# A planner's rules for shared PSUM banks and for reserved buffers, with a new list of seeds for the order of an attention stage

## Chip, cores and metric

The kernel runs on one core of a Trainium2 chip. The metric is the device time of one execution in microseconds (us); lower is better. Times are given as the median of several executions. The profile is one execution more, taken with the hardware profiler.

## The reference

Attention with a causal mask, and then two layers of matrix products with an elementwise function between the two products of each, all in fp32:

```python
scores = scale * np.matmul(q, k.transpose(0, 1, 3, 2))      # (2, 12, 448, 64) each
scores = np.where(mask, -1000000000.0, scores)
attn = np.exp(scores - np.max(scores, axis=-1, keepdims=True))
attn = attn / (np.sum(attn, axis=-1, keepdims=True) + 1e-09)
attn_out = np.matmul(attn, v)
x = attn_out.transpose(0, 2, 1, 3).reshape(896, 768)
h = x @ w_in;  x = (h * np.clip(h + 3.0, 0.0, 6.0) / 6.0) @ w_out            # 768 -> 2048 -> 768
h = x @ w2_in; y = (np.maximum(h, 0.0) + alpha * np.minimum(h, 0.0)) @ w2_out
```

## The kernel before, in words

**The two stages.** The first stage is attention. `attend` (L408) is called once for each of six groups `c`; a group has two halves, and each half (`chunks`, L497) holds two heads, one on each 64 rows of the core, called sides. TensorE (PE) makes the scores of a half in three steps (`score`, L512, tiles `s01` and `s2` of PSUM) and those of the last 64 rows of both halves of a group in one step (L436, tile `sl`). VectorE (DVE) adds the mask and takes the highest score (L463), ScalarE (ACT) takes the exponentials (L468), DVE or GpSimd (POOL) adds a constant to the sums (L483), DVE takes reciprocals (L485), and POOL or DVE scales the rows (L492; `SCALERS` = 2 leaves ACT out). PE then transposes blocks into three tiles `t` a half (L537) and, from the last rows, into two tiles `r` a group (L448). ACT or DVE copies each `t` (L563) and, for each half, its part of each `r` (L570) into the tile `a`. PE multiplies the values by `a` into a PSUM tile `o` (L581). `take_x` (L351) makes sums and differences of the `o` tiles and splits them into high and low halves (L297, L299 the high one; L303, L306 the low one), the inputs of the second stage.

The second stage is the four matrix products, each with seven block products in place of eight. All its matmuls stand on L600 in groups of three (high by high, high by low, low by high), in an order that a chain fixes. Weights arrive as 64-bit words and are turned into fp32 on ACT and DVE (L278, L281, L284). Sums of weights are made on DVE (L325) or by an accumulating DMA that POOL issues (L323).

**What sets the order.** Nothing is ordered by hand. Each step of the program is an `Op` (L50) with the engines it may run on, a duration for each, a due time, the buffers it uses and the operations that must come before it. `Plan.solve` (L117) places them one after the other: for each engine it looks at the operations that are ready, works out the earliest time `t` at which each could start (L175 to L189), and of all engines takes the earliest. Both the order on each engine and the engine of an operation that may run on several come out of this. A buffer is an object of class `Buf` (L43) and gets a slot of its class when an operation that names it is placed (L230); the slots are 8 banks of PSUM (`ps`), 12 tiles `e` and so on (`SLOTS`, L838). Before the change an operation could start only when the slot that it takes was free in time (L189), also where it only reserves the buffer for a later operation (the argument `also` of `Plan.op`, L91): the score steps on PE reserve the tile `e` that DVE writes later (L517, L519), the last-row scores reserve `el` (L440), and the transposes reserve `a` (L555). Buffers are followed by part: two engines that use different parts of one PSUM tile were not ordered by the plan. The program that is built from the plan takes a tile at the first operation that names its buffer (L888 to L902), and the framework beneath puts in the semaphores, for PSUM tiles by whole tile.

The due times of the attention operations are shifted at random by a list of seeds (`SEEDS`, L844; L131 to L142); each seed also may fix an operation to one of its engines. The first seed shifts all operations, and the others a share.

Of the kernel before, what the change touches and what calls it, by code (L numbers as in the profile page):

```python
# [42 lines left out]
class Buf:  # L43

    def __init__(self, cls, name, cols=None, dtype=None):
        self.cls, self.name, self.cols, self.dtype = cls, name, cols, dtype
        self.left, self.end, self.slot, self.tile = 0, 0.0, None, None


class Op:  # L50
# [17 lines left out]
LAG = {PE: 0.20, DVE: 0.12, ACT: 0.15, POOL: 0.10, SP: 0.04}  # L68
# [17 lines left out]
class Plan:  # L86
# [4 lines left out]
    def op(self, on, emit, reads=(), writes=(), due=FAR, chain=None, also=(), port=False, mode=None):  # L91
# [7 lines left out]
        for key in writes:  # L99
# [2 lines left out]
            o.before.update(r)  # L102
            self.state[key] = ([o], [])
        o.before.discard(o)
        for key in (*reads, *writes, *also):
            b = key[0] if isinstance(key, tuple) else key
            if b not in o.bufs:
                o.bufs.append(b)
                b.left += 1
# [7 lines left out]
    def solve(self, slots, strict, overlay, vary=0, seeds=()):  # L117
# [51 lines left out]
        while len(done) < len(self.ops):  # L169
            best = None  # L170
            room = {c: queue[c][:len(free[c])] for c in strict}
            for e in LAG:
                can = []
                for o in ready[e]:
# [7 lines left out]
                    for b in o.bufs:  # L182
                        if b.slot is None:
                            need[b.cls] = need.get(b.cls, 0) + 1
                            f = free[b.cls]
                            if len(f) < need[b.cls] or (b.cls in room and b not in room[b.cls]):
                                ok = False
                                break
                            t = max(t, sorted(f)[need[b.cls] - 1][0])  # L189
                    if ok and len(o.on) > 1:  # L190
                        def done_by(x, us):
                            late = max(clock[x], o.ready[x], port if (x == POOL and x not in o.dma) or (x == DVE and o.port) else 0.0)
# [37 lines left out]
            for b in [b for b in o.bufs if b.slot is None]:  # L230
                f = free[b.cls]
                k = min(range(len(f)), key=lambda i: f[i][0])
                b.slot = f.pop(k)[1]
                if b.cls in strict:
                    queue[b.cls].remove(b)
            for b in o.bufs:
                b.left -= 1
                b.end = max(b.end, o.out + LAG[e])
                if not b.left:
                    free[b.cls].append((b.end, b.slot))  # L240
# [600 lines left out]
SPLIT = (0, 1)  # L841
SEND = 0
SCALERS = 2
SEEDS = (13117, 66982, 68691, 27780, 6959, 27726, 88620, 72214, 67132, 73300, 90690, 68978, 52530, 59003, 43003)  # L844
ATT = {"kq": 2 * S, "v": 8 * D, "e": 3 * P, "el": 4 * P, "small": 21, "a": 16 * P}


# [5 lines left out]
def fused_kernel(ctx: ExitStack, tc: tile.TileContext, dram):  # L853
# [21 lines left out]
    with tc.manual_schedule():  # L875
# [11 lines left out]
            nc.gpsimd.memset(t[:, S:], 0.0)  # L887
        for o in order:  # L888
            for b in o.bufs:
                if b.tile is not None:  # L890
                    continue
                if b.cls == "el":
                    b.tile = last[b.slot]
# [62 lines left out]
```

## Time and profile before

| what | us |
|---|---|
| time, median of 3 runs (lowest to highest) | 500.47 (497.64 to 500.74) |
| time of the profiled execution | 497.29 |
| its span, from the first to the last instruction | 495.4 |
| PE busy in that span | 484.7 |
| mean granted clock of PE, as a share of full | 0.999 |

The span is what the trace shows; the profiled execution took 1.9 us more than its span. PE's busy time is the sum of its matmuls, whose ends are modelled. "Idle before" in a row is the time for which the engine stood before that instruction, and the name after the arrow is what ended it. The view of waits gives, for each engine, the sum of such times by line.

### The profile page before, as it was taken

What the parts mean: (1) busy time and instruction counts of PE and PEld (TensorE: products, weight loads), DVE (VectorE), ACT (ScalarE), POOL (GpSimd) and SP (SyncE); (2) the same over time, 40 slices, a digit from 0 to 9 for tenths busy, and PEclk for the clock granted to TensorE, in tenths of its full rate; (3) what the DMA queues carried; (4) which work ended last, traced back from release to release, by engine and by line L of the source; (5) the groups of instructions that cost most, each with busy time, mean ns of one, the idle gap of its engine ahead of it and who ended that gap; (6) DMA issues with size and microseconds to landing.
All of it is one profiled execution on the core that took longest, in us unless ns stands there. A gap on an engine that the chain in (4) does not pass through costs nothing.

```text
span 495.4 us, 7593 instructions
## 1 busy us (share of the span) xinstructions
PE 484.7 (98%) x2596; PEld 426.9 (86%) x2596; DVE 430.8 (87%) x823; ACT 388.4 (78%) x755; POOL 115.5 (23%) x182
## 2 busy tenths in 40 slices
PE   8899898999999999999999999999999999999997
PEld 4566576899999999999999999999999999999996
DVE  5697997999999899999999999998789988999810
ACT  5999999878989899868984578898788977697201
POOL 3767475200005001470001000121320014700000
PEclk9999999999999999999999999999999999999999
DMA  8754410334558957999105035675594689970111
GB/s 272 304 167 134 142 40 1 127 129 155 176 195 230 282 160 233 239 271 271 30 0 160 1 128 180 209 198 161 164 230 153 200 245 258 233 137 1 57 56 56
DMA packets 25334, 79.08 MB, mean 160 GB/s; under 512 B 2896, under 2 KB 13136, under 8 KB 25296
## 3 DMA queue, kind: packets, MB, share of 16 engines
q1 hardware_dynamic: 15216, 61.76, 36.3%
q0 software_dynamic: 10080, 16.85, 19.3%
q8 instruction: 20, 0.33, 0.3%
q14 instruction: 18, 0.15, 0.1%
HBM read 59.00 MB, written 2.75 MB: 125 GB/s over the span
## 4 chain that ended last, share of the span: by engine, by line
PE 91%; ACT 4%; DVE 4%; issue 1%; POOL 0%; DVEq 0%; ACTq 0%
PE ya L600 24%; PE a L600 23%; PE yc L600 12%; PE c L600 11%; PE yb L600 6%; PE b L600 6%; PE t L537 3%; PE o L581 3%; PE s L512 3%; ACT e L468 2%; ACT a L563 1%; PE warm L819 1%; DVE e L463 1%; DVE e L492 1%; PE r L448 1%
## 5 line engine op out<-in xcount | busy, mean ns | idle before, releaser
L284 DVE SCALAR_TENSOR_TENSOR wf<-wf,raw 128x768 uint32<-128x768 uint32 x64 | 60.5, 951 | 4.4 <-ACT wf L278 4.0
L323 POOL DMA_DIRECT2D g<-g x46 | 41.3, 1308 | 95.4 <-DVE x70l L306 18.6
L278 ACT ACTIVATE wf<-raw 128x768 f32<-128x768 f32 x64 | 57.9, 906 | 6.7 <-PE yc L600 3.4
L281 ACT ACTIVATE raw<-raw 128x768 uint32<-128x768 uint16 x64 | 58.6, 915 | 0.8 <-DMA raw<-w1o 0.8
L323 POOL DMA_DIRECT2D wf<-wf x17 | 16.1, 979 | 161.7 <-ACT r L676 52.2
L468 ACT ACTIVATE e<-e,small 128x384 f32<-128x384 f32 (+2 forms) x72 | 36.0, 510 | 6.2 <-DVE small L463 5.9
L463 DVE CUSTOM_DVE_ANT_0 e<-s,mask 128x384 f32<-128x384 f32 (+2 forms) x72 | 26.4, 417 | 7.6 <-PE s L512 5.5
L492 POOL TENSOR_SCALAR e<-e,small 128x256 f32<-128x256 f32 (+2 forms) x65 | 30.1, 480 | 10.9 <-DVE small L485 5.6
L581 PEld LDWEIGHTS o<-a,v 128*64 128x64 f32 x192 | 12.6, 136 | 14.0 <-issue 4.9
L581 PE MATMUL o<-a,v 128*64 128x448 f32 (+3 forms) x192 | 23.0, 385 | 1.5 <-ACT a L563 1.3
L335 ACT COPY o<-ya 128x448 f32<-128x448 f32 x3 | 1.6, 532 | 28.2 <-PE ya L600 28.2
L512 PE MATMUL s<-kq 64*128 64x256 f32 (+2 forms) x144 | 21.1, 413 | 1.0 <-DMA kq<-kq 0.7
L512 PEld LDWEIGHTS s<-kq 64*128 64x128 f32 x144 | 13.3, 195 | 9.5 <-DVE small L463 4.2
L325 DVE TENSOR_TENSOR wf<-wf 128x768 f32<-128x768 f32 (+1 forms) x23 | 19.1, 829 | 0.2
L537 PE MATMUL t<-ident,e 128*128 128x128 f32 x144 | 19.0, 277 | 0.3 <-DVE small L483 0.3
L682 ACT ACTIVATE r<-g 128x448 f32<-128x448 f32 x24 | 13.8, 575 | 6.4 <-DVE g L666 6.2
L634 DVE TENSOR_TENSOR s12l<-s,s12h 128x768 fp32r<-128x768 f32 x16 | 15.2, 951 | 3.5 <-ACT s12h L633 3.5
L676 ACT ACTIVATE r<-g 128x448 f32<-128x448 f32 x24 | 13.7, 573 | 5.6 <-DVE g L666 5.6
L537 PEld LDWEIGHTS t<-ident,e 128*128 128x128 f32 x144 | 15.6, 141 | 2.6 <-POOL e L492 1.8
L634 DVE TENSOR_TENSOR s<-wf,s 128x384 fp32r<-128x384 f32 x32 | 16.8, 548 | 0.0
L633 ACT CAST a1h<-wf 128x768 fp32r<-128x768 f32 x16 | 13.4, 837 | 3.7 <-DVE wf L284 3.6
L684 DVE SCALAR_TENSOR_TENSOR g<-r,alpha,g 128x448 f32<-128x448 f32 x24 | 16.3, 678 | 0.0
(835 smaller groups left out, 1754.5 us busy)
## 6 DMA issues: line engine op xcount, KB each, us to landing
raw<-w1i SPq DMA_DIRECT2D x16, 768.0 KB, 4.7
raw<-w1o SPq DMA_DIRECT2D x16, 768.0 KB, 5.6
raw<-w2i SPq DMA_DIRECT2D x16, 768.0 KB, 4.6
raw<-w2o SPq DMA_DIRECT2D x16, 768.0 KB, 5.7
g<-g POOLq DMA_DIRECT2D x46, 224.0 KB, 8.0
kq<-kq SPq DMA_DIRECT2D x11, 448.0 KB, 4.1
v<-v SPq DMA_DIRECT2D x12, 256.0 KB, 3.3
wf<-wf POOLq DMA_DIRECT2D x8, 384.0 KB, 10.1
```

The lines of the kernel that those rows point to most:

```text
L278: op((ACT, 0.80), lambda e: nc.scalar.activation(f32(w.tile), f32(words(1)), AF.Prelu, scale=sign * 2.0 ** -112, alpha=-2.0 ** 32), reads= ...
L281: op((ACT, 0.81), lambda e: nc.scalar.activation(words(0), raw.tile.bitcast(U16).rearrange("p (n four) -> p n four", four=4)[:, :, 1], AF. ...
L284: op((DVE, 0.87), lambda e: nc.vector.scalar_tensor_tensor(out=w.tile, in0=w.tile, scalar=3, in1=words(0), op0=ALU.logical_shift_left, op1 ...
L323: nc.gpsimd.dma_start(out=dst(), in_=src(), accum_op=ALU.add)
L463: nc.vector.tensor_tensor_reduce(out=view(), in0=t.tile[:, off:off + cols], in1=self.mask[:, at:at + cols], scale=-SCALE, scalar=3.0e38, o ...
L468: nc.scalar.activation(view(), view(), AF.Exp, bias=small.tile[:, u:u + 1], scale=-1.0, accum_out=small.tile[:, 7 + u:8 + u])
L492: (nc.gpsimd if e == POOL else nc.vector).tensor_scalar(view(), view(), by, 1.0, ALU.mult, ALU.mult)
L512: nc.tensor.matmul(t.tile[:, off:off + (i + 1) * P], lhsT=kq.tile[rows, S + i * P:S + (i + 1) * P], rhs=kq.tile[rows, 0:(i + 1) * P], star ...
L537: nc.tensor.transpose(t.tile[:, at * P:(at + 1) * P], src.tile[:, off:off + P], self.ident)
L581: nc.tensor.matmul(o.tile[side * D:(side + 1) * D, 0:cols], lhsT=v.tile[:, (2 * kc + side) * D:(2 * kc + side + 1) * D], rhs=a.tile[:, at: ...
L600: nc.tensor.matmul(out, lhsT=t.tile[:, first + at:first + at + P], rhs=rhs.tile, start=start and key is hi and rhs is xh, stop=stop and ke ...
L634: op((DVE, 0.065 + 0.00105 * cols), lambda _: nc.vector.tensor_sub(out(1), src(), f32(out(0))), reads=[*keys, parts[0][0]], writes=[parts[ ...
```

## The change

Three things change in the planner, and one in how its plan is written out. A buffer that an operation only reserves (the set `held`) still needs a slot, but its time is no longer waited for; the operation that first uses it waits for the time at which the slot came free (`b.free`). A PSUM buffer keeps, for each engine, the end of that engine's last use (`b.used`), and an operation on another engine is placed behind that end. A tile is taken at the first operation that uses its buffer, not at one that reserves it. The list of seeds is another one.

```diff
@@ class Buf
         self.left, self.end, self.slot, self.tile = 0, 0.0, None, None
+        self.free, self.used = 0.0, {}
@@ Plan.op
         o.before.discard(o)
+        o.held = {key[0] if isinstance(key, tuple) else key for key in also}
@@ Plan.solve
-                            t = max(t, sorted(f)[need[b.cls] - 1][0])
+                            if b not in o.held:
+                                t = max(t, sorted(f)[need[b.cls] - 1][0])
+                        elif b not in o.held:
+                            t = max(t, b.free)
+                        for x, end in b.used.items():
+                            if x != e:
+                                t = max(t, end + LAG[x])
@@ Plan.solve
-                b.slot = f.pop(k)[1]
+                b.free, b.slot = f.pop(k)
...
             for b in o.bufs:
+                if b.cls == "ps":
+                    b.used[e] = o.out
@@
-SEEDS = (13117, 66982, 68691, 27780, 6959, 27726, 88620, 72214, 67132, 73300, 90690, 68978, 52530, 59003, 43003)
+SEEDS = (13117, 66982, 68691, 27780, 6959, 88620, 72214, 67132, 73300, 90690, 68978, 52530, 43003, 92613, 49163, 31964, 54657, 49905, 53656, 67591, 13047, 17716, 1373, 15352, 49387, 3553, 56373, 97534, 14618, 44146, 634, 7068, 79464, 72678, 226)
@@ fused_kernel
-                if b.tile is not None:
+                if b.tile is not None or b in o.held:
                     continue
```

The lines of the changed kernel stand ten further down than those of the kernel before (L512 becomes L522, L537 L547, L581 L591, L600 L610, L563 L573, L570 L580, L448 L458, L436 L446).

The first place is PE in the middle of attention, from the fifth of the six last-row scores (`sl`) to the product `o` behind it. Before:

```order
L436 MATMUL sl<-kq 64x448 x4
L512 MATMUL s_760<-kq 128x256
L512 MATMUL s_761<-kq 128x256
L512 MATMUL s_760<-kq 128x128
L512 MATMUL s_761<-kq 128x128
L448 MATMUL r<-ident,el 128x128 x8
L537 MATMUL t<-ident,e_621 128x128
L537 MATMUL t<-ident,e_630 128x128
```

And in the changed kernel:

```order
L446 MATMUL sl<-kq 64x448 x4
L547 MATMUL t<-ident,e_616 128x128
L547 MATMUL t<-ident,e_647 128x128
L547 MATMUL t<-ident,e_631 128x128
L547 MATMUL t<-ident,e_642 128x128
L458 MATMUL r<-ident,el 128x128 x8
L547 MATMUL t<-ident,e_647 128x128
L547 MATMUL t<-ident,e_616 128x128
```

The four score matmuls between `sl` and the transposes `r` have moved behind the products `o`, and the first four of twelve transposes `t` now stand in their place.

The second place is DVE at the same time, with the rows that stand beside those of PE. Before:

```order
L563 COPY a<-t 128x2x256
L492 TENSOR_SCALAR el<-el,small 128x448
L492 TENSOR_SCALAR e_621<-e_621,small 128x128
L492 TENSOR_SCALAR e_621<-e_621,small 128x256
L463 ISA el,small<-sl,mask 128x448
L463 ISA small 128x1
L463 ISA el,small<-sl,mask 128x448
```

And in the changed kernel:

```order
L573 COPY a<-t 128x2x256
L502 TENSOR_SCALAR el<-el,small 128x448
L473 ISA el,small<-sl,mask 128x448
L473 ISA small 128x1
L473 ISA el,small<-sl,mask 128x448
L473 ISA small 128x1
L294 SCALAR_TENSOR_TENSOR wf<-wf,raw 128x768
```

The two scalings of a tile `e` that stood between the scaling of `el` and the reading of `sl` are gone from here: in the changed kernel one of them stands earlier on DVE and the other is on POOL.

The third place is PE at the end of attention, from the last four transposes `t` to the last product `o`. Before:

```order
L537 MATMUL t<-ident,e_1019 128x128
L537 MATMUL t<-ident,e_1028 128x128
L537 MATMUL t<-ident,e_1020 128x128
L537 MATMUL t<-ident,e_1023 128x128
L600 MATMUL a<-t201h,s12h 128x448
L600 MATMUL a<-t201l,s12h 128x448
L600 MATMUL a<-t201h,s12l 128x448
L581 MATMUL o<-a,v 64x448 x2
```

And in the changed kernel:

```order
L547 MATMUL t<-ident,e_1068 128x128
L547 MATMUL t<-ident,e_1098 128x128
L547 MATMUL t<-ident,e_1075 128x128
L547 MATMUL t<-ident,e_1086 128x128
L591 MATMUL o<-a,v 64x448 x2
L591 MATMUL o<-a,v 64x320 x2
L591 MATMUL o<-a,v 64x192 x2
L591 MATMUL o<-a,v 64x64 x2
```

The three matmuls of the second stage that stood between the last transposes and the last `o` have moved ahead; in the changed kernel the last `o` and the one before it each follow their own transposes directly.

## Rows read from the trace of the kernel before

**Rows 1.** The page, its head and its first part (busy time, share, instructions).

```profile
span 495.4 us, 7593 instructions
...
PE 484.7 (98%) x2596; PEld 426.9 (86%) x2596; DVE 430.8 (87%) x823; ACT 388.4 (78%) x755; POOL 115.5 (23%) x182
```

**Rows 2.** Busy time by stretch: stretch, length, each engine's busy us (instructions), clock, DMA, GB/s.

```profile
80.00:90.00 10.00, 8.69 (x62) 6.54 (x59) 9.39 (x17) 9.38 (x19) 4.40 (x5) 1.00 0.17 46
...
100.00:150.00 50.00, 50.00 (x248) 46.26 (x248) 49.00 (x82) 41.83 (x70) 0.90 (x1) 1.00 0.50 170
...
sum 95.00, PE 87.77 PEld 60.07 DVE 77.03 ACT 84.78 POOL 56.01; mean PE 4.62 PEld 3.16 DVE 4.05 ACT 4.46 POOL 2.95
```

**Rows 3.** Waits of PE in the whole span: us in total, times, longest.

```profile
PE r L448 <- POOL el L492: 1.8, 3, 1.1
PE o L581 <- ACT a L563: 1.3, 1, 1.3
PE warm L819 <- DVE mask L877: 1.3, 1, 1.3
PE r L448 <- DVE small L463: 1.1, 1, 1.1
PE s L512 <- DMA kq<-kq: 0.7, 1, 0.7
PE s L512 <- DVE small L463: 0.4, 2, 0.2
PE a L600 <- DVE a L634: 0.3, 1, 0.3
PE t L537 <- DVE small L483: 0.3, 1, 0.3
PE o L581 <- issue: 0.2, 1, 0.2
```

**Rows 4.** Waits of ACT and of DVE in the first 95 us, those between the two.

```profile
ACT a L570 <- DVE a L570: 1.2, 1, 1.2
...
ACT b2202h L297 <- DVE t L348: 0.6, 1, 0.6
...
DVE a L570 <- ACT e L468: 1.7, 1, 1.7
...
DVE t L348 <- ACT b2202h L297: 0.6, 1, 0.6
```

**Rows 5.** Timeline, 49 to 61 us: start, us, engine, line, operation, tiles, count [idle before].

```profile
49.63 0.87 DVE L492 TENSOR_SCALAR el<-el,small 128x448 f32<-128x448 f32 x1
...
50.34 1.15 POOL L306 TENSOR_TENSOR t102l<-t,t102h 128x448 fp32r<-128x448 f32 x1
50.42 1.42 DVE L492 TENSOR_SCALAR e<-e,small 128x128 f32<-128x128 f32 x2
...
50.88 0.53 ACT L299 CAST b1102h<-o 128x448 fp32r<-128x448 f32 x1
...
52.43 0.65 PE L448 MATMUL r<-ident,el 128*128 128x128 f32 x4 [1.10 <-DVE small L463]
...
60.90 1.06 PE L448 MATMUL r<-ident,el 128*128 128x128 f32 x8 [0.47 <-POOL el L492]
```

**Rows 6.** Timeline, 81 to 87 us, around the last product of attention.

```profile
81.54 1.53 PE L537 MATMUL t<-ident,e 128*128 128x128 f32 x12
...
83.39 1.56 ACT L563 COPY a<-t 128x512 f32<-128x512 f32 x3
...
85.00 1.95 PE L581 MATMUL o<-a,v 128*64 128x448 f32 x16 [1.31 <-ACT a L563]
```

**Rows 7.** ACT's groups in the first 95 us, by form: busy us, mean ns.

```profile
L563 ACT COPY a<-t 128x512 f32<-128x512 f32 x29 | 15.5, 589 | 0.2 <-PE t L537 0.2
...
L570 ACT COPY a<-r 128x256 f32<-128x256 f32 x18 | 5.9, 372 | 1.2 <-DVE a L570 1.2
```

**Rows 8.** The page, accumulating DMA issues: KB each, median us to landing.

```profile
g<-g POOLq DMA_DIRECT2D x46, 224.0 KB, 8.0
```

## The prediction, made before the changed kernel ran

> **What bounds the kernel now.** I read the first part of the page before anything else, since it says how much there is to win. PE is busy for 484.7 us of a span of 495.4 us [rows 1], so all its idle time is 10.7 us, 2.2% of the span. Then I cut the span into stretches. From 100 us on PE is busy for all of each of the seven stretches of 50 us up to 450 us, of which one is shown [rows 2]; the order of PE's matmuls there is the same before and after the change, matmul by matmul. Whatever the change wins or loses, it does so in the first 95 us, the attention stage.
>
> The third view is the list of PE's waits, which accounts for the 10.7 us. The first matmul stands for 1.3 us until its operand is set, which no order of attention can change. The other eight lines add up to 1.8 + 1.3 + 1.1 + 0.7 + 0.4 + 0.3 + 0.3 + 0.2 = 6.1 us [rows 3]. The rest, 10.7 - 1.3 - 6.1 = 3.3 us, lies behind the last matmul (copies and stores). The 6.1 us are the ceiling of the gain: the same PE instructions run before and after, and no PE work is removed.
>
> The fourth view says who keeps PE waiting. Over those 95 us ACT is busy for 84.8, DVE for 77.0 and PE for 87.8 us [rows 2]. Three engines are nearly full at once, so a wait that leaves PE can come back on another engine's queue. From 80 to 90 us DVE and ACT are each busy for 9.4 of 10 us, and PE only for 8.7 [rows 2]: at the end of attention PE follows the other two.
>
> A measurement of this kernel can tell about 1%, which is 5 us here. That is nearly the whole ceiling.
>
> **The change part by part.** The change adds no instruction of a new kind; it moves instructions, and some from one engine to another. I go through the stage in order of time, and give each part a value and two ends.
>
> The start, to 24 us. Here lie the wait for the first load (0.7), one wait of `r` for POOL's scaling of `el` (1.1, with 0.2 behind it, both within the 1.8), one of `t` (0.3), one of `s` (0.2) and one of `o` (0.2) [rows 3]: 2.7 us. The new order puts one scaling of a 128x384 tile on POOL ahead of that of `el`, and takes a smaller operation away from DVE ahead of its reciprocal. The two are of one size, about 0.6 us, going by the two scalings of 1.42 us in the row on DVE [rows 5], which I take as a bound. Value 0, ends -0.6 and +0.6.
>
> The middle, 49 to 61 us. Before, four transposes `r` stand for 1.10 us because their bank still holds `sl`, which DVE has not read [rows 5]. DVE is late because it scales `el` (0.87 us) and two tiles `e` (1.42 us) first [rows 5]. In the new order the two tiles `e` are gone from between, so DVE reads `sl` 1.4 us sooner, and PE has four transposes `t` to do meanwhile. The 1.10 us should go. The next stop is the 0.47 us before the eight `r` at 60.90 us, which wait for POOL's scaling of the next `el` [rows 5]. There POOL issued an accumulating DMA ahead of the scaling and now issues it behind; ACT takes the exponentials of `el` right behind its copies, ahead of the casts. I take 1.3 of the 1.57 us as won, with ends of -1.6 and 0: at 0, the scores that moved behind `o` run when DVE is full again, and their reading is the next thing that is late.
>
> The end of attention, 62 to 87 us. Before, one `o` stands for 1.31 us, until ACT has copied the three transposed tiles [rows 6], and one `s` for 0.2 us. The three copies take 1.56 us and began 1.9 us behind the start of the twelve transposes, although three matmuls of the second stage stood between; ACT had other work queued ahead [rows 6]. In the new order the last two `o` both follow their own transposes without anything between, and all their copies are on ACT, also behind other work of ACT. If ACT's queue is clear, only the last copy shows: 0.59 us [rows 7]. If it is not, the wait is as before plus the time of the three matmuls that stood between, some 0.6 us (248 instructions fill 50 us [rows 2], so 0.2 us each): 1.31 + 0.6 = 1.9 us. Two of them are 1.2 to 3.8 us, where 1.5 stood before. I take 1.1 for each, nearer to the lower end because ACT is relieved: it does two casts of 0.53 us and two copies of `r` of 0.37 us less, and one copy of `t` of 0.59 us more [rows 5, 7], which is -1.2 us. Value 2.2 - 1.5 = +0.7, ends -0.3 and +2.3.
>
> The last wait is of 0.3 us for a low half of weights on DVE [rows 3]. That subtraction stood behind a sum on the last `o` and two sums of hidden rows, and in the new order it stands ahead of the latter two. I take -0.3, with ends of -0.3 and 0.
>
> The plan's bank rule. Where two engines use one PSUM tile, the program already makes one wait for the other: ACT's copy of `r` stood for 1.2 us until DVE's copy of the same `r` was over, DVE's for 1.7 us behind ACT's, and the casts and sums on `o` for 0.6 us each way [rows 4]. This adds no wait to the program; it lets the plan see those that are there, and in the new order three of four copies of an `r` mostly follow one another on ACT. These 4.1 us are on engines that hold PE only at times, and what they give PE is within the parts above. The reservations cost nothing before on the chip either, since no matmul writes an `e` or `a` tile; what goes is a rule of the plan.
>
> The second stage. Five sums of weights or of hidden rows go from DVE to DMAs that POOL issues. Such a transfer lands 8.0 us behind its issue [rows 8]. PE had no wait at all in that stage, so I take 0; one that comes too late would cost up to its 8.0 us.
>
> Sum: 0 - 1.3 + 0.7 - 0.3 = -0.9 us; with the ends of each part from -2.8 to +2.9.
>
> The Trainium skill has a rule that speaks against the middle part. The row shows the scaling of a 128x448 `el` on DVE at 0.87 us while POOL works on SBUF too [rows 5]. "SBUF — State Buffer", section "Who interferes with whom", says that a DVE instruction with two inputs in SBUF, and one in a mode that uses two ports, contends with GpSimd, and that the one that comes later stands until the other is done. The new order moves such two-input instructions (the joining of weight words and two sums) right behind the reading of `sl`, beside POOL's 1.15 us subtraction [rows 5]. By that rule DVE could lose up to 1.15 us there, the reciprocal of the next `el` would be as late, and the middle part would give -0.2 in place of -1.3; the sum would be +0.2. By the rows alone it stays at -0.9.
>
> The profiled execution took 497.29 us. The four times known are 497.29, 497.64, 500.47 and 500.74: two pairs 3 us apart, with no cause in the profile. The median given, 500.47, is in the upper pair. A new median can fall in either, so I set the sum against the middle of the four, (497.64 + 500.47) / 2 = 499.1 us: 499.1 - 0.9 = 498.2 us. On the profiled execution's own time it is 496.4 us.
>
> **The rivals.** First, slower: the end of attention takes more than the middle gives. It has one place, the last two `o`. What speaks for it is that ACT and DVE are full there [rows 2] and that the one such `o` before did wait [rows 6]; against it, ACT's 1.2 us less. At 1.9 us each the end gives +2.3, and if POOL and DVE win only 0.5 us in the middle, since PE then meets the same full engines sooner, the sum is +2.3 - 0.5 - 0.3 = +1.5 us: 500.6 us. It decides when each of the two waits is over 1.6 us.
>
> Second, a true gain: with the bank waits of ACT and DVE planned for, the 4.1 us between them [rows 4] go, both engines run ahead, and PE's waits behind 24 us all go: 6.1 - 2.7 = 3.4 us. That is 495.7 us. For it speaks that three engines are full at once, so time saved on ACT is soon time saved on PE; against it, that PE's own waits have other causes named (a late scaling, a copy).
>
> Third, the new order is only another order: what PE does not wait for here it waits for there, because the work of ACT and DVE is the same to about 1 us. The sum is 0: 499.1 us. This case and my forecast can't be told apart by time.
>
> Fourth, a transfer of the second stage comes late and PE stands for 8.0 us: 507 us. PE's empty list there speaks against it.
>
> **How the numbers follow.** My forecast (a gain of 0 to 2 us) gets 0.42, the third rival 0.20, the slower one 0.18, the true gain 0.17, the late transfer 0.03. The range: its lower end is the lower pair with two thirds of the true gain, 497.3 - 2.3 = 495.0; its upper end is the upper pair with the slower case, 500.7 + 1.5 = 502.2. Faster by over 1% would need 5 us of 6.1, or the true gain together with a median that falls in the lower pair: 0.09. Slower by over 1% needs the late transfer, or the slower case at its end in an upper pair: 0.05. The rest, 0.86, is within 1%.
>
> **What would show it right or wrong.** In the profile of the changed kernel, PE is busy for 484 to 486 us and without a wait from 100 us on. The wait of `r` for DVE's reading is gone or under 0.3 us. There are two waits of `o` for ACT's copies near the end, of about 1 us each. ACT's busy time in the first 95 us is about 1 us less. The last stretch without gaps begins within 2 us of where it did. I am wrong if PE's idle time outside start and end falls below 3 us or rises above 9, or if PE waits in the second stage.

## The result, and the profile after

| | before | after |
|---|---|---|
| time, median of 22 runs each (lowest to highest) | 499.13 us (496.83 to 502.24) | 495.00 us (493.66 to 502.35) |
| span of the profiled execution | 495.4 us | 491.9 us |
| start of the second `o` | 22.74 us | 22.15 us |
| end of ACT's last three copies `a<-t` | 84.95 us | 82.51 us |
| start of the second matmul group on `b1100` | 95.55 us | 92.46 us |

The ratio is 0.9914, with a 95% interval of 0.9888 to 0.9939: the changed kernel is faster by about 4 us, just under 1%. The times of the kernel before lie in two groups some 3 us apart (eleven of 22 between 496.8 and 497.8 us, the others at 500.5 and above), those of the changed kernel spread over three (fourteen at 493.7 to 495.8 us, three at 497.0 to 499.3, five at 501.4 and above), and the ratio leaves out these five and none of the other kernel's, so I also compare the lowest times: 493.66 against 496.83, 3.2 us. The spans differ by 3.5 us.

The page of the changed kernel, head and first part, which answers to [rows 1]:

```profile
span 491.9 us, 7617 instructions
...
PE 484.0 (98%) x2596; PEld 428.1 (87%) x2596; DVE 428.6 (87%) x821; ACT 387.2 (79%) x752; POOL 121.4 (25%) x187
```

PE is idle for 7.9 us of the span, where it was 10.7. All waits of PE in the changed kernel (us in total, times, longest), which answer to [rows 3]:

```profile
PE r L458 <- POOL el L502: 1.6, 2, 1.4
PE warm L829 <- DVE mask L887: 1.3, 1, 1.3
PE o L591 <- ACT a L573: 1.3, 2, 1.1
PE t L547 <- POOL el L502: 0.2, 1, 0.2
```

Beside the wait for the mask at the start that is 3.1 us in place of 6.1. The second stage has no wait, as before.

The larger surprise stands on ACT. Its waits of 0.2 us and more between 10 and 92 us were 1.2 and 0.6 us at banks shared with DVE [rows 4], 1.3 us in two for DVE's reading of scores, and two of 0.2 us. In the changed kernel one is left:

```profile
ACT r L686 <- DVE g L676: 0.5, 1, 0.5
```

To see what that is worth I take one stretch of both kernels: from the start of the second `o` on PE to the end of ACT's last three copies, behind which the last `o` of attention runs. Busy time of each engine in it (stretch, length, then PE, PE's weight loads, DVE, ACT, POOL; clock, DMA, GB/s), before:

```profile
22.74:84.95 62.21, 59.19 (x464) 40.81 (x464) 52.98 (x184) 59.56 (x183) 42.32 (x79) 1.00 0.32 97
```

And after:

```profile
22.15:82.51 60.36, 58.93 (x465) 40.79 (x464) 52.17 (x186) 59.95 (x182) 43.57 (x79) 1.00 0.36 114
```

ACT's work in it grew by 0.39 us (59.56 to 59.95), the time it stands fell from 62.21 - 59.56 = 2.65 us to 0.41 us, and the stretch became 1.85 us shorter: -2.24 + 0.39. In the changed kernel ACT hardly stops. This led to the theory that the experiments put to the test. The sum itself proves nothing, since it can be written for any engine: for PE it is -1.59 us of standing (3.02 to 1.43) and -0.26 us of work (59.19 to 58.93).

Where the 3.5 us of the span come from: 0.59 us up to the second `o`, 1.85 us in this stretch, 0.65 us from there to the second group on `b1100` (22.15 + 60.36 + 9.95 = 92.46, before 22.74 + 62.21 + 10.60 = 95.55), and 0.4 us behind it that no wait shows.

### The profile page after: what moved, and what is told of

Read it like the earlier page. It is cut to its first block, busy times and chain, and to the rows that moved or that the text cites. A ratio compares the mean times of both kernels' runs of the same rounds, so it can differ in the third digit from the quotient of the medians.

```text
span 491.9 us, 7617 instructions
## 1 busy us (share of the span) xinstructions
PE 484.0 (98%) x2596; PEld 428.1 (87%) x2596; DVE 428.6 (87%) x821; ACT 387.2 (79%) x752; POOL 121.4 (25%) x187
## 4 chain that ended last, share of the span: by engine, by line
PE 94%; ACT 2%; POOL 1%; DVE 1%; issue 0%; POOLq 0%
PE ya L610 24%; PE a L610 24%; PE c L610 12%; PE yc L610 12%; PE yb L610 6%; PE b L610 6%; PE o L591 4%; PE t L547 3%; PE s L522 2%; PE r L458 1%; PE sl L446 1%; POOL e L502 1%; ACT a L573 1%; POOL el L502 1%; DVE e L473 0%; DVE el L473 0%
## 5 line engine op out<-in xcount | busy, mean ns | idle before, releaser
L333 POOL DMA_DIRECT2D g<-g x48 | 43.1, 1228 | 94.9 <-DVE x70l L316 18.7
L294 DVE SCALAR_TENSOR_TENSOR wf<-wf,raw 128x768 uint32<-128x768 uint32 x64 | 61.5, 966 | 4.7 <-ACT wf L288 4.4
L333 POOL DMA_DIRECT2D wf<-wf x19 | 17.7, 929 | 148.6 <-ACT r L686 52.4
L502 POOL TENSOR_SCALAR e<-e,small 128x256 f32<-128x256 f32 (+2 forms) x67 | 31.4, 487 | 10.3 <-DVE small L495 3.3
L591 PE MATMUL o<-a,v 128*64 128x448 f32 (+3 forms) x192 | 23.4, 386 | 1.3 <-ACT a L573 1.3
L591 PEld LDWEIGHTS o<-a,v 128*64 128x64 f32 x192 | 12.5, 136 | 13.3 <-issue 4.6
L522 PE MATMUL s<-kq 64*128 64x384 f32 (+2 forms) x144 | 20.9, 417 | 0.0
L522 PEld LDWEIGHTS s<-kq 64*128 64x128 f32 x144 | 13.7, 201 | 7.1 <-issue 1.4
L547 PE MATMUL t<-ident,e 128*128 128x128 f32 x144 | 18.9, 277 | 0.2 <-POOL el L502 0.2
L547 PEld LDWEIGHTS t<-ident,e 128*128 128x128 f32 x144 | 15.6, 141 | 3.3 <-POOL e L502 1.6
L335 DVE TENSOR_TENSOR wf<-wf 128x768 f32<-128x768 f32 (+1 forms) x21 | 18.0, 857 | 0.3
L573 ACT COPY a<-t 128x512 f32<-128x512 f32 x30 | 16.1, 591 | 0.2
```

Of the source, the lines that this page charges most:

```text
L294: op((DVE, 0.87), lambda e: nc.vector.scalar_tensor_tensor(out=w.tile, in0=w.tile, scalar=3, in1=words(0), op0=ALU.logical_shift_left, op1 ...
L333: nc.gpsimd.dma_start(out=dst(), in_=src(), accum_op=ALU.add)
L502: (nc.gpsimd if e == POOL else nc.vector).tensor_scalar(view(), view(), by, 1.0, ALU.mult, ALU.mult)
L522: nc.tensor.matmul(t.tile[:, off:off + (i + 1) * P], lhsT=kq.tile[rows, S + i * P:S + (i + 1) * P], rhs=kq.tile[rows, 0:(i + 1) * P], star ...
L547: nc.tensor.transpose(t.tile[:, at * P:(at + 1) * P], src.tile[:, off:off + P], self.ident)
L591: nc.tensor.matmul(o.tile[side * D:(side + 1) * D, 0:cols], lhsT=v.tile[:, (2 * kc + side) * D:(2 * kc + side + 1) * D], rhs=a.tile[:, at: ...
```

## The experiments

Each kernel ran beside the kernel before on the same chip. The lowest time of each kernel stands beside its ratio; the kernel before had lowest times of 497.08 to 497.35 us in these comparisons. "Stretch" is the one defined above. The letters of the theories hold within one round of experiments: those of `b_swap`, `b_one`, `b_both` and `b_act`, written first, are not those of the later ones. From the second round on, theory A is that ACT's queue sets the end of attention, so that each microsecond in which ACT works or stands there is paid in full; rival C is that PE's waits have a cause each, and no engine bounds the stage.

**Two sums more of work on ACT or on DVE.** `b_act` and `a_act` add two copies of 128x448 on ACT to the kernel before and to the changed one; `b_dve` and `a_dve` add two sums of the same size on DVE (0.62 us each) in the same way. Nobody reads what they write.

```diff
     order = solve(k)
+    at = next(i for i, o in enumerate(order) if o.eng == ACT and o.start > 30.0)
+    for _ in range(2):
+        extra = Op([(ACT, 0.57)], lambda e: nc.scalar.copy(k.scratch, k.mask[:, 0:S]), 0.0)
+        extra.eng = ACT
+        order.insert(at, extra)
...
```

> The kernel before with two more ACT instructions at about 30 us (copies of 128x448 within SBUF into a tile that nobody reads, about 0.57 us each, 1.15 us together). If ACT is the engine that sets the end of the stage before the change, the mark of 95.55 us comes 1.0 to 1.2 us later; if ACT has room (it waits 1.2, 0.9, 0.6, 0.6 and 0.4 us behind 50 us), at most 0.4 us later. The same two instructions are put into the changed kernel, whose ACT hardly waits: there 0.9 to 1.2 us if ACT is the bound, at most 0.4 if not.

> The changed kernel with two more copies of 128x448 on ACT at about 30 us (1.15 us in all), whose result nobody reads. Theory A, ACT sets the end of attention in the changed kernel (it stands for only 0.9 us between 10 and 96 us): the second matmul group on b1100 begins 0.9 to 1.2 us later than its 92.46 us, and the time is 0.9 to 1.2 us longer. Rival C, each of PE's waits has a cause of its own and no engine bounds the stage as a whole: 0.2 to 0.6 us, part of it lost in waits of ACT that get shorter.

> The kernel before with two more sums of 128x448 on DVE at about 30 us (1.2 us in all), whose result nobody reads. Theory A, ACT sets the end and DVE has room (it stands for 12.4 us between 10 and 92 us before): 0 to 0.3 us later than 95.55 us. Rival C, DVE is as much a cause of PE's waits as ACT (the wait of r for DVE of 1.1 us, ACT's waits for DVE at shared tiles of 2.4 us): 0.8 to 1.2 us later.

> The changed kernel with the same two sums on DVE at about 30 us (1.2 us). Theory A: 0 to 0.3 us later than 92.46 us, since DVE still stands for some 9.9 us between 10 and 92 us. Rival C: 0.8 to 1.2 us, since with ACT's waits for DVE planned away the two engines hang together more closely.

Measured, the stretch in each (ACT's idle time is the length less its busy time):

| kernel | stretch | ACT busy | ACT idle | change of the stretch | lowest time | ratio (95% interval) |
|---|---|---|---|---|---|---|
| before | 62.21 | 59.56 | 2.65 | | | |
| `b_act` | 63.31 | 60.65 | 2.66 | +1.10 | 498.02 | 0.9999 (0.9955 to 1.0043) |
| `b_dve` | 63.24 | 59.76 | 3.48 | +1.03 | 498.28 | 1.0010 (0.9977 to 1.0043) |
| after | 60.36 | 59.95 | 0.41 | | | |
| `a_act` | 61.40 | 60.97 | 0.43 | +1.04 | 494.76 | 0.9923 (0.9883 to 0.9963) |
| `a_dve` | 61.15 | 60.19 | 0.96 | +0.79 | 494.02 | 0.9918 (0.9882 to 0.9954) |

The expectations name another mark, the start of the second group on `b1100`. It came 1.04 us later in `b_act` and 1.07 in `b_dve`, 1.29 in `a_act` and 0.77 in `a_dve`.

On ACT the added 1.1 us show in full, before the change as well as after it, although ACT stood for 2.65 us in the stretch before: its waits absorb nothing of work added at 30 us, the one place tried. That is what theory A says. On DVE theory A expected next to nothing, because DVE stands for 9.2 us of the stretch, and it was wrong: DVE's 1.2 us cost 1.03 and 0.79, about what rival C expected (0.8 to 1.2). The rows of `b_dve` show the way that this takes. Its stretch:

```profile
22.77:86.01 63.24, 59.96 (x464) 40.98 (x464) 53.78 (x186) 59.76 (x183) 42.13 (x79) 1.00 0.31 95
```

ACT works as much as before there and stands 0.83 us longer. ACT's waits in `b_dve` from 22 to 92 us:

```profile
ACT a L570 <- DVE a L570: 1.2, 1, 1.2
ACT a L563 <- PE t L537: 0.9, 2, 0.8
ACT b2202h L297 <- DVE t L348: 0.6, 1, 0.6
ACT e L468 <- DVE small L463: 0.5, 2, 0.2
```

The wait of ACT for PE's transposes grew from 0.2 to 0.9 us: a late DVE reaches ACT through the engines between. So ACT is on the chain that sets the end of attention (the row of steps in which each starts when the one before it is done), and DVE reaches it too; the runs do not show that ACT alone sets it, and none added work to POOL.

PE's rows hide this loss. In `a_act` PE stands in the stretch for 1.44 us, as in the changed kernel (1.43), and its busy time is 1.03 us longer (59.96 for 58.93) with the same 465 matmuls. It lies in one row of scores behind the added copies (start, us, tiles, count), in the changed kernel and in `a_act`:

```profile
33.18 1.66 PE L522 MATMUL s<-kq 64*128 64x128 f32 x12
...
33.29 2.73 PE L522 MATMUL s<-kq 64*128 64x128 f32 x12
```

The same twelve matmuls take 1.07 us longer, and all that follows in the stretch is as much later. So the list of PE's waits does not hold all that PE loses in attention, and its sum is no ceiling of a gain.

**One part of the new order at a time.** `b_swap` moves the two scalings of `e` on DVE behind the two readings of `sl`, the edit on which the prediction's middle part rests:

```diff
     order = solve(k)
+    moved = order[357], order[359]
+    order = order[:357] + [o for o in order[358:366] if o not in moved] + list(moved) + order[366:]
```

`b_one` takes the bank waits away from ACT: copies of one `r` go to one engine, and the two casts of one `o` (the high half on ACT, the low half on DVE) move behind ACT's last three copies. `b_both` has both edits; `b_one2` and `b_both2` are the same two kernels again.

```diff
+    order[372].eng = order[159].eng = ACT
+    order[163].eng = DVE
+    cast = order[584], order[589]
+    last = max(i for i, o in enumerate(order[:605]) if o.eng == ACT and any(x.cls == "a" for x in o.bufs))
+    order = [o for o in order[:last + 1] if o not in cast] + list(cast) + order[last + 1:]
```

> The kernel before, with two instructions moved: DVE's two scalings of a tile e at 50 us stand behind its reading of the last-row scores, not ahead of it. The mark is the start of the second block row of the second stage (the matmul a<-b1100h by a1h that comes the second time): 95.55 us before, 92.46 after, so 3.1 us to explain. Theory A (PE's own waits, taken one by one, are the loss): the 1.10 us wait of r goes, and the mark comes 0.8 to 1.1 us earlier. Theory B (ACT and DVE hold one another at shared PSUM tiles, and a wait taken from PE alone comes back later): the wait of r goes, but the o that waited 1.31 us waits for longer, and the mark moves by 0.4 us or less.

> The kernel before, with the places changed at which ACT and DVE wait for one another at a PSUM tile: each of the two r tiles of two groups is copied by one engine (one copy goes from DVE to ACT, two copies change engines), and the high half of b2202 with its low half stands behind the last three copies of t on ACT. Theory A: no wait of PE is removed but part of the 1.31 us of the last o (ACT starts those copies about 1 us sooner); the mark of 95.55 us comes 0.5 to 1.0 us earlier. Theory B: ACT's waits of 1.2 and 0.6 us go, ACT runs that much ahead from 54 us on, and the mark comes 1.2 to 2.0 us earlier.

> The kernel before with both edits: the two scalings moved, and no PSUM tile read by ACT and DVE in turn at those places. Theory A: the sum of the two, 1.3 to 2.1 us earlier than 95.55. Theory B: more than the sum of the two, 2.0 to 3.0 us, since either edit alone only moves the wait to the other engine.

> The kernel of b_one once more. From the start of the second o to the end of ACT's last three copies the kernel before takes 62.21 us, of which ACT works 59.56 and stands 2.65 us. Theory A, ACT's queue sets the end and what it does not stand is won: ACT stands 1.0 to 1.6 us and the length is 60.6 to 61.2 us. Rival C, ACT's waits for DVE at shared banks are paid for elsewhere: length within 0.3 us of 62.21 us.

> The kernel of b_both once more. Theory A: ACT stands under 1 us and the length from the second o to the end of ACT's last three copies is 60.0 to 60.6 us, where the changed kernel has 60.36 us. Rival C: 61.0 us or more.

| kernel | stretch | ACT busy | ACT idle | change of the stretch | lowest time | ratio (95% interval) |
|---|---|---|---|---|---|---|
| `b_swap` | 61.29 | 59.63 | 1.66 | -0.92 | 496.64 | 0.9977 (0.9940 to 1.0014) |
| `b_one2` | 61.72 | 59.64 | 2.08 | -0.49 | 497.26 | 1.0029 (0.9984 to 1.0073) |
| `b_both2` | 60.89 | 59.53 | 1.36 | -1.32 | 499.96 | 1.0035 (0.9986 to 1.0084) |

The first profiles of `b_one` and `b_both` began with a stretch at a lower granted clock (last section), so that their second `o` came a microsecond late; their lengths (61.50 and 59.95 us) are left out of the table. Their ratios are 0.9991 (0.9949 to 1.0034) and 0.9970 (0.9930 to 1.0011), their lowest times 497.47 and 496.63 us.

In all three ACT's work is the same to 0.1 us, and the stretch is shorter by what ACT stands less. The two edits about add up (-0.92 and -0.49 make -1.41, measured -1.32). The lengths of `b_one2` and `b_both2` miss what theory A expected by 0.5 and 0.3 us and rival C's by 0.2 and 0.1, because a wait that goes is in part replaced. In `b_one2` the 1.8 us at banks are gone, and ACT's waits from 22 to 92 us begin with three others:

```profile
ACT a L570 <- PE r L448: 0.7, 1, 0.7
ACT e L468 <- DVE small L463: 0.5, 2, 0.2
ACT el L468 <- DVE small L463: 0.4, 1, 0.4
```

PE's last `o` waits 0.17 us there in place of 1.31 [rows 6], but counted from the second `o` it begins only 0.48 us sooner (61.78 us for 62.26):

```profile
84.96 1.95 PE L581 MATMUL o<-a,v 128*64 128x448 f32 x16 [0.17 <-ACT a L563]
```

`b_swap` is not an edit of PE's wait alone. ACT's 1.2 us at a bank shrinks in it too, so most of that wait had come from the same late DVE:

```profile
ACT a L570 <- DVE a L570: 0.3, 1, 0.3
```

And the two scalings of `e`, which took 1.42 us from 50.42 us on, beside POOL's subtraction of 1.15 us [rows 5], take 0.54 us in `b_swap`, from 52.04 us on, when that subtraction (50.87 to 52.03) is over. So 0.9 us of DVE's time went with the move, and the run does not part that from the order.

At the mark of the expectations, 95.55 us before, less is left: 95.09 in `b_swap`, 96.17 in `b_one2` and 95.13 in `b_both2` (96.61 in `b_one`, 95.15 in `b_both`), outside what both theories of the first round expected of `b_swap`, `b_one` and `b_both`. Part of this is the start: up to the second `o` these kernels and the one before have one order, and it begins at 22.67 to 23.21 us. From the second `o` on the mark is 0.93 us earlier in `b_swap`, 0.18 later in `b_one2` and 0.65 earlier in `b_both2`; in the changed kernel it is 2.50 us earlier.

Of the time nothing measurable came of `b_one`, and 0.7 us of `b_swap` (496.64 against 497.35 us); in `b_one`, with the casts moved behind the copies, the second stage waits 0.5 us for a sum on DVE (`PE a L600 <- DVE g L666`), which PE did not do before. In the profile of `b_both2` the matmuls of one layer took 2% longer (last section), so its time says little on the edits; `b_both` won 0.7 us by lowest times, as `b_swap` did alone. The two edits together give 1.3 of the 1.85 us of the changed kernel in the stretch, and half of that is lost behind it.

**The three matmuls at the end.** `a_end` puts the three matmuls on `t201` of the changed kernel back between the last twelve transposes and the last `o`.

```diff
     order = solve(k)
+    order = order[:561] + order[562:592] + [order[561]] + order[592:]
```

> The changed kernel with the three matmuls of the second stage on t201 put back to where the kernel before had them, between the last twelve transposes and the last o. The prediction held that an o straight behind its transposes pays 0.6 us more than one with these three between, so moving them should be worth up to 0.6 us on the last o (its wait 1.05 to 0.45 us) and cost up to 0.6 us on the o before it (0.24 to 0.85 us). Theory A, ACT's queue alone sets when the last three copies are over: the last o begins where it did (82.57 us within 0.2), and the time stays within 0.3 us. Rival C: it moves by the sum of the two, between -0.4 and +0.4 us.

PE at the end of attention in `a_end` (start, us, tiles, count, idle before):

```profile
77.58 1.95 PE L591 MATMUL o<-a,v 128*64 128x448 f32 x16 [0.56 <-ACT a L573]
...
82.01 1.24 PE L591 MATMUL o<-a,v 128*64 128x448 f32 x6 [0.42 <-ACT a L573]
```

The two waits were 0.24 and 1.05 us, so each moved by the 0.3 to 0.6 us of the matmuls in front of it. The stretch stayed at 60.28 us (60.36), ACT busy 59.89 of it. The lowest time is 493.10 us, the ratio 0.9906 (0.9870 to 0.9941). Counted from the span's start the last `o` came 0.56 us sooner (82.01), which neither theory expected, but the second `o` was 0.47 us sooner already; from there it is 60.33 us to the last `o`, for 60.42. Where PE's matmuls stand changes PE's waits and not the end, as theory A has it.

**Rules and search apart.** The planner's rules and its seeds changed together. To part them, seeds were searched anew for each of four sets of rules, with three searches of 4,000 lists each: neither rule (`f_old`, `g_old`), banks alone (`f_bank`, `g_bank`), reserved tiles alone (`f_held`, `g_held`), both (`f_both`, `g_both`). `f` is the plan that the planner rates best of the three searches of its set, `g` one from another search. For banks alone the planner has, out of the diff shown ahead, only these lines on what is waited for:

```diff
+                        for x, end in b.used.items():
+                            if x != e:
+                                t = max(t, end + LAG[x])
```

> The planner of the kernel before (neither rule), with its order searched anew: the best of three searches of 4000 seeds each by the planner's own estimate. Theory R, the rule on banks is what pays, since a plan that does not see these waits lets ACT stand on the chip: ACT waits for DVE at shared banks for 1.5 us or more between 22 and 92 us, and the time is 495.5 to 498 us where the kernel before takes 497.5. Rival S, any fresh search of this size finds what the new order found: 493 to 495 us, with ACT's bank waits under 0.5 us.

> The rule on banks alone (tiles only reserved are still waited for in the plan), searched with the same effort. Theory R: no wait of ACT for DVE at a shared bank over 0.3 us, the second group on b1100 begins at 91 to 93 us, the time is 492.5 to 494.5 us. Rival S: no better than the searched order without either rule, within 0.7 us.

> The rule on reserved tiles alone (the plan does not see that engines at one bank follow one another), searched with the same effort. Theory R: as with neither rule, 495 to 498 us, ACT stands 1.5 us or more at shared banks. Rival S: 493 to 495 us.

> Both rules, as in the changed kernel, with an order from the same search as the other three. Theory R and rival S both: 492.5 to 494.5 us, as the changed kernel or up to 1.2 us faster; the rule on banks without the one on reserved tiles is within 0.7 us of it if the latter is worth nothing on the chip, as the prediction held.

> Neither rule, with the order of another search of 4000 seeds. Theory R, the rule on banks makes the difference, since a plan that does not see the waits at shared banks leaves them to the chip: 495 to 498.5 us, and between 10 and 92 us ACT and DVE wait for one another for 1.5 us or more. Rival L, the orders differ by luck only: anywhere from 492.5 to 496.5 us, with no split between the two pairs.

> The rule on banks alone, with the order of another search. Theory R: 492.5 to 495 us, ACT and DVE wait for one another for under 1.3 us between 10 and 92 us. Rival L: anywhere from 492.5 to 496.5 us.

> The rule on reserved tiles alone, with the order of another search. Theory R: 495 to 498.5 us, waits of ACT and DVE for one another of 1.5 us or more. Rival L: anywhere from 492.5 to 496.5 us.

> Both rules, with the order of another search. Theory R: 492.5 to 494.5 us, waits of ACT and DVE for one another under 1.3 us. Rival L: anywhere from 492.5 to 496.5 us.

| kernel | bank rule | ACT idle, 10 to 92 us | lowest time | median | ratio (95% interval) |
|---|---|---|---|---|---|
| `f_both` | yes | 0.16 | 492.51 | 492.63 | 0.9905 (0.9889 to 0.9920) |
| `f_bank` | yes | 1.38 | 492.97 | 493.35 | 0.9917 (0.9901 to 0.9933) |
| after | yes | 0.87 | 493.66 | 495.00 | 0.9914 (0.9888 to 0.9939) |
| `g_bank` | yes | 0.69 | 493.67 | 493.81 | 0.9885 (0.9751 to 1.0019) |
| `g_both` | yes | 3.47 | 494.31 | 496.60 | 0.9924 (0.9861 to 0.9986) |
| `f_old` | no | 1.84 | 494.55 | 495.67 | 0.9952 (0.9909 to 0.9994) |
| `f_held` | no | 4.01 | 495.55 | 496.12 | 0.9965 (0.9937 to 0.9992) |
| `g_old` | no | 3.68 | 496.58 | 498.54 | 0.9983 (0.9934 to 1.0031) |
| `g_held` | no | 3.13 | 496.75 | 497.17 | 0.9959 (0.9915 to 1.0003) |
| before | no | 4.10 | 497.10 | 497.82 | |

By lowest time the eight new orders split: the four with the rule on banks average 493.4 us, the four without it 495.9 us. Were the rule of no use, four given ones of eight would be the fastest four once in 70 times. The gap between the two sets is narrow, 0.24 us (`g_both`, `f_old`), and by medians `g_both` falls among those without the rule. A fresh search without the rule wins 0.3 to 2.6 us on the kernel before, 1.2 us on average, so the search has a share too; `f_old`, at a lowest time of 494.55 us, came in the range of rival S. The rule on reserved tiles shows no effect that can be told from that of a search (0.5 us better to 1.0 us worse in the four pairs), as the prediction held.

ACT's idle time orders the ten kernels nearly as their times do (the profiles of `g_both` and `g_old` have a stretch at a lower clock). That is agreement and no proof: DVE stands less in that window as well, 12.4 us before, 9.9 in the changed kernel and 5.4 in `f_both`. `f_both`, page head and PE busy time:

```profile
span 491.0 us, 7583 instructions
...
PE 483.0 (98%) x2596; PEld 425.6 (87%) x2596; DVE 436.8 (89%) x849; ACT 387.8 (79%) x752; POOL 101.8 (21%) x159
```

ACT in `f_both` from 10 to 92 us (stretch, length, busy time):

```profile
10.00:92.00 82.00, 81.84 (x240) 1.00 0.45 152
```

It is the fastest order of this study, 1.1 us below the changed kernel by lowest times, and ACT stands in it for only 0.16 us of this window.

One expectation failed: without the rule the waits at banks were to be 1.5 us and more on ACT itself. In `f_old` they are 0.6 us, in `f_held` 0.3 us. There they sit on DVE, whose waits from 10 to 92 us in `f_held` include four behind ACT:

```profile
DVE a L577 <- ACT e L475: 1.0, 1, 1.0
DVE a L577 <- ACT a1h L640: 0.8, 1, 0.8
...
DVE t L355 <- ACT b2202h L304: 0.6, 1, 0.6
...
DVE a L577 <- ACT a L577: 0.2, 1, 0.2
```

And ACT, in the same kernel and stretch, stands 2.3 us for DVE's reading of scores:

```profile
ACT e L475 <- DVE small L470: 2.3, 2, 2.2
```

That the second follows from the first fits `b_dve`; no run took it apart. Waits of either engine for the other at shared banks, added up in that window without the low halves, which need the high half anyway, are 0 in `f_bank`, `f_both` and `g_both` and 0.9 us in `g_bank`; without the rule they are 0.6 us in `f_old`, 1.3 in `g_old`, 1.5 in `g_held` and 2.9 in `f_held`. So the rule does take them out of the orders, but `f_old` has less of them than `g_bank` and is slower: how the rule makes an order faster is shown only in part.

## Why the prediction was wrong in size

The direction, the place (attention, nothing in the second stage) and the middle part were right; the forecast of -0.9 us was too small by 2.6 us of span, and the median of 495.00 us lies at the lower end of its range. The rival called the true gain (-3.4 us, 495.7 us), with a chance of 0.17, came nearest in number. Its mechanism came true in part: the waits of ACT and DVE at shared banks are gone, but of PE's 3.4 us of waits behind 24 us 1.5 are left, and the start, from which it took nothing, gave a share. That its number fits is in part luck.

In the prediction's own terms, PE's listed waits, the start gave -1.1 us (2.7 to 1.6, of which 0.7 is chance, see below) where 0 was forecast, the middle -1.6 for -1.3, the end of attention 0.0 for +0.7, the last wait -0.3 as forecast: together -3.0 for -0.9. The other 0.5 us of the span are in no wait: PE's busy time fell by 0.7 us, and the time behind the last matmul grew by 0.2. Of the signs that it named, the wait of `r` for DVE is gone and PE waits nowhere behind 100 us, as forecast; the two waits of `o` are 0.24 and 1.05 us for about 1 each.

The step that failed is the pricing of PE's waits place by place, each as a cost of its own, with ACT's and DVE's waits at banks put at nothing; by it the end came out at +0.7 for 0.0. The start is a second miss, a term put at 0 that gave 0.6 to 0.7 us (below). Three runs show that such a wait is no price. `a_end` moves the three matmuls for which the prediction charged 0.6 us: the waits change by 0.3 and 0.6 us, and the last `o` begins, counted from the second, within 0.1 us of where it did. In `b_one2` the wait of the last `o` falls by 1.1 us, and that `o` begins 0.5 us sooner. In `a_act` PE loses 1.04 us in the stretch, and its waits there do not grow. What the runs show in its place is that the copies `a<-t` on ACT, for which the last `o` waits, set its start, and that 1.1 us of work added on ACT, or 1.2 on DVE, delays them by 0.8 to 1.1 us. The forecast priced how long PE would stand there; when ACT would be done entered it only as a relief of ACT by 1.2 us, which did not come.

The middle. Forecast -1.3 us, measured -1.57: both stops are gone. PE and DVE there after the change, which answers to [rows 5]:

```profile
48.61 0.66 PE L547 MATMUL t<-ident,e 128*128 128x128 f32 x4
48.80 0.60 DVE L473 CUSTOM_DVE_ANT_0 el<-sl,mask 128x448 f32<-128x448 f32 x1
49.10 1.04 PE L458 MATMUL r<-ident,el 128*128 128x128 f32 x8
...
49.81 1.14 POOL L316 TENSOR_TENSOR t102l<-t,t102h 128x448 fp32r<-128x448 f32 x1
...
49.88 1.88 DVE L294 SCALAR_TENSOR_TENSOR wf<-wf,raw 128x768 uint32<-128x768 uint32 x1
...
56.82 1.09 PE L458 MATMUL r<-ident,el 128*128 128x128 f32 x8
```

DVE reads `sl` right behind its scaling of `el`, PE does four `t` meanwhile, and neither `r` waits. The joining of weight words on DVE took 1.88 us beside POOL's subtraction, where its mean is 0.97 us: those are the 0.9 us longer which the rule of the Trainium skill ("SBUF — State Buffer", section "Who interferes with whom") made possible in the prediction. The trace agrees with the rule, but nothing that PE waited for stood behind it.

The end of attention. Forecast +0.7 us, from two `o` at 1.1 us each, less 1.5. Measured: 0.24 + 1.05 = 1.29 us, and 0.2 us of a `t` for POOL's scaling of `el`, which is new: 1.5 us, a change of 0.0. PE and ACT there, which answers to [rows 6]:

```profile
76.83 1.03 PE L547 MATMUL t<-ident,e 128*128 128x128 f32 x8
...
77.47 1.07 ACT L573 COPY a<-t 128x512 f32<-128x512 f32 x2
78.10 1.95 PE L591 MATMUL o<-a,v 128*64 128x448 f32 x16 [0.24 <-ACT a L573]
...
80.92 1.59 ACT L573 COPY a<-t 128x512 f32<-128x512 f32 x3
...
82.57 1.95 PE L591 MATMUL o<-a,v 128*64 128x448 f32 x16 [1.05 <-ACT a L573]
```

The last copies begin 0.94 us behind their transposes (79.98 to 80.92) where it was 1.85 us (81.54 to 83.39, [rows 6]). I had read the latter as ACT's queue being full. Two thirds of the difference was a bank wait just ahead of these copies. ACT in the kernel before:

```profile
82.94 0.55 ACT L297 ACTIVATE b2202h<-o 128x448 fp32r<-128x448 f32 x1 [0.62 <-DVE t L348]
```

That wait stood in [rows 4], and I put it among those on engines that "hold PE only at times", and did not ask whether ACT, the engine named in PE's row, could have been earlier. These waits by themselves are not the missing gain either: `b_one2`, without 1.8 us of them, gained 0.49 us in the stretch and nothing at the second stage. That ACT does less work (1.2 us by the prediction) was wrong as well: in the stretch its work grew by 0.39 us, and in the first 95 us from 84.8 to 88.8 us, since work of the second stage comes sooner.

The start. Forecast 0, with ends of 0.6 either way; measured -0.59 at the second `o`. The waits of `t` and `s` for DVE are gone, and the one of `r` for POOL is longer (1.6 us in two, for 1.1 + 0.2). Six profiles of the old order at the start and four of the new one, where no lower clock fell in, have the second `o` at 22.67 to 23.21 and at 21.68 to 22.26 us. What moves it within either set lies ahead of the first waiting `r`: from the start of that `r` to the second `o` the old order takes 9.00 to 9.03 us in all six, the new one 8.31 to 8.34 in all four. So 0.7 us of gain there is real, and the waits of `t`, `s` and `o` (0.3, 0.2 and 0.2 us) are nearly all of it; no run put them back one by one. That the wait for the first load (0.7 us) is missing in the changed kernel's profile is chance, since PE waits for 0.6 to 1.3 us in that part in the other three profiles of the new start.

The last wait of 0.3 us went as forecast, and the second stage stayed without a wait.

Why the program waits at shared banks at all: the Trainium skill ("PSUM — Partial Sum Buffer", section "PSUM bank collisions raise a hardware error") holds that two engines must not touch one bank in the same 32 partitions at the same time, reads against reads included. The traces show the waits (1.2 us before a copy of `r`, which only reads that bank); no run here tried to do without them.

Left open: 0.4 us behind the second group on `b1100` are in no wait, and what part of the gap between the two edits (1.3 us in the stretch, 0.65 at the second stage) and the whole order (1.85 and 2.50 us) is due to which further move was not taken apart.

## What to carry to other kernels

When several engines are nearly full, do not price a change by the waits of one of them. A wait that goes can come back elsewhere, and a loss can hide in rows that count as busy. Take the stretch that bounds the kernel and see for every engine how its work and its standing change. That length is work plus standing is true of any engine, so the sum alone does not say which one counts; adding a known 1 us of idle work to an engine tells in one run whether that engine is on the chain at that place, and more than one can be. A planner that lacks a wait which the program must make leaves it to chance where it falls; orders searched with the rule were on average 2.5 us faster here than orders searched as long without it, and the fresh search alone gave 1.2 us.

## What the runs showed beside this

**Two paces of the same matmuls.** In some profiles one of the two layers of the second stage runs 2% slower at a granted clock of 1.00. The first and the last group of 72 matmuls on the chain of `b_both2`:

```profile
186.56 14.88 PE ya L600 x72
...
451.15 14.59 PE yc L600 x72
```

In the changed kernel's profile the first such group takes 14.59 us too. In `b_one2` this cost 3.4 us: its second group on `b1100` begins 0.62 us later than in the kernel before, its last group of 72 matmuls 4.00 us later. The slower pace came with either order, on the first layer in `a_act`, `b_one`, `b_one2` and `b_both2`, and on the second in `b_both`; no cause was found in the profile.

**A dip of the clock at the start.** In four profiles (`b_one`, `b_both`, `g_old`, `g_both`) the granted clock falls to a mean of 0.66 from 15 to 20 us. PE in `g_both` by stretch (length, busy time and matmuls, clock, DMA share, GB/s):

```profile
10.00:15.00 5.00, 4.28 (x34) 1.00 1.03 414
15.00:20.00 5.00, 3.85 (x20) 0.66 0.94 386
20.00:25.00 5.00, 5.00 (x41) 1.00 0.24 74
```

Ahead of the dip PE was busy for 4.28 of 5 us in `g_both` and for 2.92 in `g_old`; the changed kernel was busy for 3.41 us there and kept 1.00. A mean of 0.66 is a part of the stretch at the lower level of 1.2 GHz.
